# Attention with a learned position bias and a soft mixture of experts on one core: the last bias rows stored in two steps, and a 64-row bias tile read with a doubled source

## The chip, the core and the metric

One core of a Trainium2 chip runs the whole program. Its engines are PE (matmul; its weight loads are shown as PEld), DVE (vector), ACT (scalar), POOL and SP, whose queue issues every transfer of this kernel. The metric is the time on the device in microseconds, less is better.

## The reference

`q`, `k`, `v` have 8 batches, 8 heads, 576 positions and 64 dimensions. The position bias comes out of a small network with 32 hidden units and one output per head:

```python
scores = scale * np.matmul(q, k.transpose(0, 1, 3, 2))
x = (psi_rel / psi_i)[..., None]          # log1p(|i - j|) / log1p(max(i, 1))
h = np.maximum(x @ w1 + b1, 0.0)
bias = h @ w2
scores = scores + bias.transpose(2, 0, 1)[None, :, :, :]
attn = np.exp(scores - np.max(scores, axis=-1, keepdims=True))
attn = attn / (np.sum(attn, axis=-1, keepdims=True) + 1e-09)
out = np.matmul(attn, v)
```

The bias is the same for all batches and differs by head. The output of attention, 4608 tokens of 512, then goes through a soft mixture of 8 experts with 4 slots each: softmax over the tokens gathers slots, each expert is a two-layer network with weights 512 x 1024 and 1024 x 512, and a softmax over the slots spreads the results back.

## The kernel before

**Order.** Each step of the program has a name and a place in `ORDER` (line 23), a list written out by hand; steps are recorded with `step` and emitted in that order, engine by engine. A plus behind a place chooses the other engine for a step. The step `f28.3/-1` is job 28's fourth f tile, `t4.00/8` a step of unit 8.

**Bias jobs.** The bias of row i and column j depends on i and |i - j|, so 16 rows of one block make a strip of 591 values per row and head. There are 36 jobs, 8 for each block of 128 rows and 4 for the last 64 rows (`bias_job`, line 887). A job has four f tiles (ACT line 900 or DVE line 902), a product on PE (line 911) and one e tile of 128 rows (16 positions x 8 heads) x 591 (ACT line 921). Step D stores the e tile, 295.5 KB, to `bias_m` or `bias_r` in device memory (line 927). Jobs 24 to 31 make the fourth block of 128 rows, jobs 32 to 35 the last 64 rows. f and e tiles share 25 buffers (`W1N`); a buffer is free again when its last reader is done, for an e tile its store.

**Units.** A unit is one pair of heads and one batch; the 8 batches of a pair follow each other, so unit 8 begins the second pair. A unit has four blocks of 128 rows, and units of even number a fifth, the last 64 rows of two batches together in one tile of 128 partitions. For each block, PE makes scores (line 439, the fifth block line 444), DVE adds the bias and takes the extreme (line 459), ACT takes exp (line 468), POOL scales (line 374), PE transposes (line 423), and products with `v` follow (line 547).

**Bias loads.** `load_bias` (line 357) reads the bias of one pair: a bm tile of 128 rows x 1152 for each of blocks 0 to 3 (steps b0 to b3) and a br tile for the last 64 rows (b4). Both batches need the same 64 rows, so br holds them twice, in partitions 0 to 63 and 64 to 127. A tile is read in three pieces, 576 columns of the first head, then the last 64 and the first 512 of the second (line 355). The first pair's loads stand among the bias jobs' stores on SP; the other pairs' loads stand in the last units of the pair before.

**SP** works strictly in order. A load that waits for its store, or for its buffer, holds up all behind it. `load_qk` (line 343) and `load_v` (line 348) fetch the inputs of a unit into two buffers each, and `fetch_w` (line 874) fetches expert weights (wt) ahead.

Of the kernel before, what the change touches and what calls it, by code (L numbers as in the profile page):

```python
# [53 lines left out]
e4.0/2 S2.0/3 t0.10/3 m4/2 e1.0/3 t0.00/3 S2.1/3 n4.1/2 e1.1/3 t0.11/3 t2.00/3 n4.0/2 t0.01/3 t2.10/3 e0.1/3 M0/2
e0.0/3 t2.01/3 T4/2 R4/2 S3.0/3 m1/3 cR4/2+ n1.1/3 c4/2 S3.1/3 M1/2 t2.11/3 n1.0/3 Mr/2 t3.10/3 t3.11/3 t3.00/3 e2.1/3
m0/3 n0.1/3 n0.0/3 e2.0/3 e3.1/3 t3.01/3 e3.0/3 m2/3 xs/0 R1/3 xs/1 n2.0/3 x0/2 T1/3 lq/4 x1/2+ T0/3 cR1/3 m3/3 c1/3
S1.0/4 t1.10/4 t1.00/4 c0/3 n2.1/3 S1.1/4 T2/3 t1.01/4 n3.1/3 n3.0/3 lq/5 t1.11/4 S0.0/4 c2/3 S0.1/4 t0.00/4 e1.0/4
R3/3 cR3/3 T3/3 t0.10/4 t0.11/4 t0.01/4 S2.0/4 S3.0/4 c3/3 e0.0/4 e1.1/4 S3.1/4 t2.00/4 t3.00/4 t2.10/4 t3.10/4 S2.1/4
# [170 lines left out]
def body(ctx, tc, qk, v, wcol, phi, mw1, mw2, tabh, consth, *outs):  # L229
    nc = tc.nc  # L230
    P = 128
    S, D = 576, 64
# [119 lines left out]
    def read_bias(out, src, h, j0, j1):  # L352
        (row, n), (head, _), _ = src.ap
        x = bass.AP(src.tensor, src.offset + head * h + n - 1 + j0, [[row - 1, n], [1, j1 - j0]])
        nc.sync.dma_start(out=out, in_=x)
# [857 lines left out]
```

## Time and profile before

| what | value |
|---|---|
| median of 3 runs | 583.6 us (582.7 to 585.42) |
| the profiled execution | 582.65 us |
| its span, first to last instruction | 580.9 us |
| PE, DVE, ACT, POOL busy | 95%, 78%, 79%, 38% of the span |
| device memory read, written | 81.25 MB, 27.41 MB |

Times in rows of the profile are microseconds from the start of the span. A row of a timeline shows start, length, engine, line, operation, output and inputs, and in brackets the idle time of the engine just before and what ended it. SPq rows are issues of transfers; "x6" counts what is merged in a row. A row of the windows view shows a stretch, busy time of the five engines, then the granted clock of PE, the mean busy share of the 16 DMA engines and the GB/s they moved. A row of the DMA view ends with the median time from issue to landing.

### The profile page before, as it was taken

What the parts mean: (1) busy time and instruction counts of PE and PEld (TensorE: products, weight loads), DVE (VectorE), ACT (ScalarE), POOL (GpSimd) and SP (SyncE); (2) the same over time, 40 slices, a digit from 0 to 9 for tenths busy, and PEclk for the clock granted to TensorE, in tenths of its full rate; (3) what the DMA queues carried; (4) which work ended last, traced back from release to release, by engine and by line L of the source; (5) the groups of instructions that cost most, each with busy time, mean ns of one, the idle gap of its engine ahead of it and who ended that gap; (6) DMA issues with size and microseconds to landing.
All of it is one profiled execution on the core that took longest, in us unless ns stands there. A gap on an engine that the chain in (4) does not pass through costs nothing.

```text
span 580.9 us, 19319 instructions
## 1 busy us (share of the span) xinstructions
PE 549.4 (95%) x7367; PEld 354.8 (61%) x7367; DVE 454.4 (78%) x1811; ACT 459.2 (79%) x959; POOL 217.9 (38%) x308
## 2 busy tenths in 40 slices
PE   5989899999999999999999999999999999989993
PEld 3445566667766666666776666676666666543661
DVE  7998778788889788787788888888897889761333
ACT  6979889988888998988988889888879788431232
POOL 4000455555545554455544554545235331400000
PEclk9999799999999999999999999999999999999997
DMA  5598523153865254777522266430543534699978
GB/s 158 217 317 292 175 63 104 62 186 129 292 182 193 71 176 131 277 203 276 166 88 87 85 202 179 153 111 35 175 146 124 171 129 150 252 401 409 392 290 317
DMA packets 44301, 109.91 MB, mean 189 GB/s; under 512 B 8496, under 2 KB 8880, under 8 KB 44208
## 3 DMA queue, kind: packets, MB, share of 16 engines
q1 hardware_dynamic: 44208, 108.67, 54.5%
q8 instruction: 58, 0.95, 0.7%
q14 instruction: 35, 0.29, 0.2%
HBM read 81.25 MB, written 27.41 MB: 187 GB/s over the span
## 4 chain that ended last, share of the span: by engine, by line
PE 68%; DVE 11%; ACT 8%; DMA 6%; issue 4%; POOL 2%; SPq 0%; DVEq 0%; ACTq 0%; POOLq 0%
PE ps L439 18%; PE ps L547 16%; PE ps L423 14%; DVE y L459 6%; PE ps L911 4%; PE ps L444 3%; DMA xo<-xs 3%; ACT y L468 3%; PE ps L557 3%; PE ps L1037 2%; PE ps L986 2%; ACT f L900 2%; DMA qk<-in_qk_dram 2%; POOL y L374 2%; PE ps L1070 2%
## 5 line engine op out<-in xcount | busy, mean ns | idle before, releaser
L374 POOL TENSOR_SCALAR y<-y,sm 128x576 f32<-128x576 f32 x288 | 210.4, 746 | 274.8 <-DVE sm L476 220.9
L468 ACT ACTIVATE y<-y,mn 128x576 f32<-128x576 f32 x288 | 220.8, 770 | 21.2 <-DVE mn L459 16.0
L439 PE MATMUL ps<-qk 64*128 64x288 f32 x1024 | 161.3, 424 | 1.7 <-DMA qk<-in_qk_dram 0.9
L377 ACT COPY at<-ps 128x1024 f32<-128x1024 f32 (+2 forms) x151 | 132.1, 895 | 22.9 <-PE ps L423 18.8
L547 PE MATMUL ps<-at,v 128*64 128x320 f32 (+1 forms) x1024 | 133.7, 410 | 0.2 <-ACT y L468 0.2
L459 DVE CUSTOM_DVE_ANT_0 y<-ps,bm,mn 128x288 f32<-128x288 f32 x256 | 123.5, 512 | 8.8 <-PE ps L439 3.4
L423 PEld LDWEIGHTS ps<-ident,y 64*128 64x128 f32 x2592 | 100.5, 139 | 42.7 <-POOL y L374 17.0
L459 DVE CUSTOM_DVE_ANT_0 y<-ps,bm 128x288 f32<-128x288 f32 x256 | 108.2, 453 | 15.9 <-PE ps L439 9.2
L423 PE MATMUL ps<-ident,y 64*128 64x64 f32 x2592 | 113.6, 227 | 3.2 <-DVE mn L459 1.0
L439 PEld LDWEIGHTS ps<-qk 64*128 64x128 f32 x1024 | 101.3, 188 | 19.4 <-DVE mn L459 2.9
L547 PEld LDWEIGHTS ps<-at,v 128*64 128x64 f32 x1024 | 69.9, 137 | 54.5 <-DVE mn L459 6.5
L468 ACT ACTIVATION_READ_ACCUMULATOR y<-y,mn 128x1 f32 x288 | 54.8, 190 | 0.0
L475 DVE TENSOR_SCALAR sm<-sm 128x2 f32<-128x2 f32 x144 | 36.1, 251 | 20.7 <-ACT y L468 20.3
L911 PE MATMUL ps<-f,wbd 128*32 128x79 f32 (+44 forms) x640 | 44.1, 403 | 6.6 <-DVE f L902 3.9
L902 DVE TENSOR_SCALAR f<-tabs,scl,nb 128x560 f32<-128x560 f32 (+17 forms) x106 | 46.0, 507 | 2.9 <-DMA bias_m<-e 1.0
L459 DVE DVE_READ_ACCUMULATOR2_ANT mn<- 128x1 f32 x576 | 47.6, 83 | 0.0
L911 PEld LDWEIGHTS ps<-f,wbd 128*32 128x32 f32 x640 | 22.0, 113 | 28.9 <-issue 9.9
L377 DVE COPY at<-ps 128x1024 f32<-128x1024 f32 (+2 forms) x41 | 31.2, 763 | 5.4 <-PE ps L423 4.4
L900 ACT ACTIVATE f<-tabs,cols,scl 128x432 f32<-128x432 f32 (+15 forms) x38 | 26.4, 748 | 2.4 <-DMA bias_m<-e 2.4
L476 DVE RECIPROCAL sm<-sm 128x2 f32<-128x2 f32 x144 | 23.9, 166 | 4.9
L921 ACT ACTIVATE e<-ps,bcon 128x591 f32<-128x591 f32 x36 | 25.8, 762 | 1.1 <-PE ps L911 1.1
L557 PE MATMUL ps<-at,v 64*64 64x320 f32 x128 | 23.9, 448 | 0.0
(152 smaller groups left out, 434.9 us busy)
## 6 DMA issues: line engine op xcount, KB each, us to landing
wt<-in_moe_w_dram SPq DMA_DIRECT2D x62, 512.0 KB, 7.2
qk<-in_qk_dram SPq DMA_DIRECT2D x32, 576.0 KB, 4.3
bias_m<-e SPq DMA_DIRECT2D x32, 295.5 KB, 3.6
v<-in_v_dram SPq DMA_DIRECT2D x32, 288.0 KB, 4.5
xs<-xts SPq DMA_DIRECT2D x24, 288.0 KB, 3.6
xo<-xs SPq DMA_DIRECT2D x8, 864.0 KB, 4.9
bm<-bias_m SPq DMA_DIRECT2D x16, 288.0 KB, 4.4
bm<-bias_m SPq DMA_DIRECT2D x16, 256.0 KB, 4.5
```

The source lines that it names most:

```text
L374: nc.gpsimd.tensor_scalar(out=out, in0=y, scalar1=r, scalar2=1.0, op0=ALU.mult, op1=ALU.mult)
L377: (nc.vector.tensor_copy if eng else nc.scalar.copy)(out=out, in_=in_)
L423: nc.tensor.matmul(out, src[rs], ident[rs, rs], is_transpose=True, start=True, stop=True, tile_position=(64 * r, 0))
L439: nc.tensor.matmul(pss[hh].t[:, 0:HALF], x[rs, S + p * P:S + (p + 1) * P], x[rs, k0:k0 + HALF], start=True, stop=True, tile_position=(64 * ...
L459: nc.vector.tensor_tensor_reduce(out=d["y", p][:, hs], in0=d["ps", p, n][hh].read()[:, 0:HALF], in1=biases[hp][p][:, hs], scale=-QS, scala ...
L468: nc.scalar.activation(out=y, in_=y, func=AF.Exp, bias=d["mn", p][:, 2 + hh:3 + hh], scale=-1.0, accum_out=d["sm", p][:, hh:hh + 1])
L475: nc.vector.tensor_scalar(out=r, in0=r, scalar1=1e-9, scalar2=None, op0=ALU.add)
L547: nc.tensor.matmul(po.t[o:o + 64, 0:wide[c]], d["v"][:, 64 * (4 * hh + i):64 * (4 * hh + i) + 64], main[:, :, 4 * hh + i, :], start=i == 0 ...
L557: nc.tensor.matmul(d["po", c].t[o:o + 64, 0:wide[c]], d["v"][rs, 512:576], keys[c][rs], start=False, stop=True, tile_position=(64 * hh, o))
L900: nc.scalar.activation(out=f, in_=tabs[:, 0:n], func=AF.Relu, bias=cols[:, 1:2], scale=sc)
L902: nc.vector.tensor_scalar(out=f, in0=tabs[:, 0:n], scalar1=sc, scalar2=nb1[:, 0:1], op0=ALU.mult, op1=ALU.max)
L911: nc.tensor.matmul(pb.t[32 * t:32 * t + 32, a // 512, a % 512:a % 512 + c1 - c0], wbd, x, start=True, stop=True, tile_position=(0, 32 * t))
```

## The change

Three things are changed.

1. For jobs 24 to 35, step D stores only the rows of the first two heads (the first pair), in two transfers of 16 rows x 591. A new step H stores the whole e tile again, as D did before. The twelve H steps stand in `ORDER` behind `lq/3`, the load of the fourth batch's q and k.
2. The br tile is read in three transfers rather than six. The source has a leading step of zero and a count of 2, so one transfer writes all 128 partitions.
3. Jobs 0 to 23 are unchanged.

```diff
-c3/1 S2.0/2 S2.1/2 S1.1/2 t2.00/2 S3.0/2 e0.1/2 t2.10/2 S3.1/2 t2.11/2 e0.0/2 t1.11/2 m0/2 e1.1/2 t3.00/2 M1/1 t1.01/2
+H24/-1 H25/-1 H26/-1 H27/-1 H28/-1 H29/-1 H30/-1 H31/-1 H32/-1 H33/-1 H34/-1 H35/-1 c3/1 S2.0/2 S2.1/2 S1.1/2 t2.00/2
...
-    def read_bias(out, src, h, j0, j1):
+    def read_bias(out, src, h, j0, j1, twice=False):
         (row, n), (head, _), _ = src.ap
-        x = bass.AP(src.tensor, src.offset + head * h + n - 1 + j0, [[row - 1, n], [1, j1 - j0]])
+        x = bass.AP(src.tensor, src.offset + head * h + n - 1 + j0, [[0, 2]] * twice + [[row - 1, n], [1, j1 - j0]])
         nc.sync.dma_start(out=out, in_=x)
...
             x = bsp.tile([P, 2 * S], F32, name="bm", tag="bm")
-            read_bias(x[:, 0:S], bias_m[c], h0, 0, S)
-            read_bias(x[:, S:S + 64], bias_m[c], h0 + 1, 512, S)
-            read_bias(x[:, S + 64:], bias_m[c], h0 + 1, 0, 512)
+            src = bias_m[c], False
         else:
             x = bsp.tile([P, 2 * S], F32, name="br", tag="br", bufs=1)
-            for r in range(2):
-                rs = slice(64 * r, 64 * r + 64)
-                read_bias(x[rs, 0:S], bias_r, h0, 0, S)
-                read_bias(x[rs, S:S + 64], bias_r, h0 + 1, 512, S)
-                read_bias(x[rs, S + 64:], bias_r, h0 + 1, 0, 512)
+            src = bias_r, True
+        read_bias(x[:, 0:S], src[0], h0, 0, S, src[1])
+        read_bias(x[:, S:S + 64], src[0], h0 + 1, 512, S, src[1])
+        read_bias(x[:, S + 64:], src[0], h0 + 1, 0, 512, src[1])
...
+    LATE = 24
...
-        step(-1, f"D{i}", lambda _: nc.sync.dma_start(out=dst, in_=d["e"]))
+        every = dst.rearrange("p h j -> (p h) j")
+        def store(_):
+            nc.sync.dma_start(out=every, in_=d["e"])
+        def first_pair(_):
+            for h in range(2):
+                nc.sync.dma_start(out=every[h::H], in_=d["e"][h::H])
+        if i < LATE:
+            step(-1, f"D{i}", store)
+        else:
+            step(-1, f"D{i}", first_pair)
+            step(-1, f"H{i}", store)
```

On PE, DVE, ACT and POOL the same instructions stand in the same order. SP's order changes, and with it which buffer an f or e tile gets and for whom it waits.

SP before, at the end of the bias jobs (the last stores, the loads of bm and br for the first pair, then the third and fourth batches' qk and v):

```order
L927 DMA bias_m<-e 128x591 x4
L927 DMA bias_r<-e 128x591 x3
L355 DMA bm<-bias_m 128x576
L355 DMA bm<-bias_m 128x64
L355 DMA bm<-bias_m 128x512
L355 DMA br<-bias_r 64x576
L355 DMA br<-bias_r 64x64
L355 DMA br<-bias_r 64x512
...
L343 DMA qk<-in_qk_dram 128x1152 x2
L348 DMA v<-in_v_dram 128x576 x2
```

SP in the changed kernel, at the same place:

```order
L934 DMA bias_m<-e 16x591 x8
L934 DMA bias_r<-e 16x591 x6
L356 DMA bm<-bias_m 128x576
L356 DMA bm<-bias_m 128x64
L356 DMA bm<-bias_m 128x512
L356 DMA br<-bias_r 128x1x576
L356 DMA br<-bias_r 128x1x64
L356 DMA br<-bias_r 128x1x512
L344 DMA qk<-in_qk_dram 128x1152 x2
L930 DMA bias_m<-e 128x591 x8
L930 DMA bias_r<-e 128x591 x4
L349 DMA v<-in_v_dram 128x576 x2
```

Seven whole stores ahead of the loads have become fourteen small ones, br has half the transfers, and twelve whole stores stand between the qk and the v loads.

ACT before, in the bias jobs' second half, with the semaphores that each instruction waits for (a name with DMAHW is a transfer; the row of 128x384 is the step f23.3):

```order
L900 ACTIVATE f<-tabs,cols,scl 128x480 [waits DMAHW6_49,DVE_49]
L921 ACTIVATE e<-ps,bcon 128x591 [waits PE_49,Activation_49]
L921 ACTIVATE e<-ps,bcon 128x591 [waits DMAHW1_49,DVE_49,PE_49]
L900 ACTIVATE f<-tabs,cols,scl 128x384 [waits DMAHW2_49,Activation_49]
...
L900 ACTIVATE f<-tabs,cols,scl 128x448 [waits DVE_49]
...
L900 ACTIVATE f<-tabs,cols,scl 128x528
```

ACT in the changed kernel, the same instructions:

```order
L900 ACTIVATE f<-tabs,cols,scl 128x480 [waits PE_49]
L921 ACTIVATE e<-ps,bcon 128x591 [waits DVE_49,PE_49]
L921 ACTIVATE e<-ps,bcon 128x591 [waits DMAHW0_49,PE_49]
L900 ACTIVATE f<-tabs,cols,scl 128x384 [waits Activation_49]
...
L900 ACTIVATE f<-tabs,cols,scl 128x448 [waits DMAHW2_49]
...
L900 ACTIVATE f<-tabs,cols,scl 128x528 [waits DMAHW0_49]
```

The steps of 128x480 and 128x384 no longer wait for a store, those of 128x448 and 128x528 now do.

More of the change, by code (lines that the diff above doesn't have):

```diff
@@ L54 @@
[L54 to L58, printed above, removed]
@@ new lines @@
+S1.1/4 T2/3 t1.01/4 n3.1/3 n3.0/3 lq/5 t1.11/4 S0.0/4 c2/3 S0.1/4 t0.00/4 e1.0/4 R3/3 cR3/3 T3/3 t0.10/4 t0.11/4
+t0.01/4 S2.0/4 S3.0/4 c3/3 e0.0/4 e1.1/4 S3.1/4 t2.00/4 t3.00/4 t2.10/4 t3.10/4 S2.1/4 e0.1/4 m1/4 M1/3 lv/4 t3.11/4
+t3.01/4 n1.0/4 t2.11/4 n1.1/4 m0/4 e3.1/4 M0/3 n0.0/4 e3.0/4 e2.1/4 t2.01/4 e2.0/4 T1/4 n0.1/4 m3/4 T0/4 n3.1/4 R1/4
+n3.0/4 Mr/3 c1/4 cR1/4+ S4.0/4 c0/4 S4.1/4 m2/4 x0/3+ x1/3 t4.10/4 t4.00/4 T3/4 xs/3 n2.0/4 S1.0/5 t4.11/4 t4.01/4
+c3/4 S2.0/5 n2.1/4 R3/4 t1.10/5 t1.00/5 lq/7 S2.1/5 xs/2 cR3/4 S1.1/5 t2.10/5 t2.00/5 e4.0/4 e4.1/4 T2/4 S0.0/5
@@ new lines @@
+t3.01/6 e0.1/6 t2.10/6 m0/6 M1/5 n0.0/6 t3.11/6 n0.1/6 e3.0/6 e3.1/6 n1.0/6 t2.11/6 lv/6 T0/6 t2.00/6 b0/7 R1/6 Mr/5
+t2.01/6 m3/6 cR1/6+ S4.0/6 e2.1/6 e2.0/6 S4.1/6 c0/6 m2/6 x1/5+ n2.1/6 T1/6 x0/5 S0.0/7 t4.10/6 t4.00/6 S0.1/7 n3.1/6
+t4.11/6 t4.01/6 c1/6 S1.0/7 n2.0/6 t0.10/7 e4.1/6 t0.00/7 t0.11/7 n3.0/6 e4.0/6 lq/8 lv/7 t0.01/7 T3/6 R3/6 xs/5
+t1.10/7 cR3/6 m4/6 t1.00/7 S1.1/7 T2/6 S3.0/7 c3/6 n4.1/6 n4.0/6 t1.11/7 c2/6 S3.1/7 t1.01/7 S2.0/7 b2/7 t3.10/7
+e1.1/7 t3.00/7 R4/6 cR4/6+ t3.11/7 T4/6 e0.1/7 c4/6+ e0.0/7 e1.0/7 t2.00/7 S2.1/7 M0/6 m0/7 t3.01/7 lq/9 n0.0/7 M1/6
@@ new lines @@
+c0/8 t4.00/8 t4.10/8 t4.11/8 T1/8 t4.01/8 n3.0/8 n3.1/8 T2/8 c1/8 R3/8 cR3/8 S1.0/9 c2/8+ lv/8 T3/8 S0.0/9 S0.1/9
+t1.10/9 e4.1/8 c3/8 t1.00/9 e4.0/8 S1.1/9 t0.00/9 t0.10/9 t0.01/9 m4/8 n4.0/8 t0.11/9 e0.0/9 S2.0/9 S2.1/9 e0.1/9
+t1.01/9 t1.11/9 t2.00/9 m0/9 e1.0/9 n4.1/8 t2.10/9 M0/8 n0.0/9 lq/10 T4/8 R4/8 t2.01/9 S3.0/9 e1.1/9 n0.1/9 cR4/8+
+c4/8 S3.1/9 t2.11/9 T0/9 m1/9 n1.1/9 t3.00/9 t3.10/9 e2.0/9 n1.0/9 c0/9+ t3.11/9 w0/8 t3.01/9 M1/8 e2.1/9 R1/9 lv/9
+m2/9 T1/9 cR1/9+ n2.0/9 S0.0/10 S0.1/10 e3.1/9 w0/12 Mr/8 e3.0/9 m3/9 t0.10/10 t0.00/10 c1/9 n2.1/9 S1.0/10 lq/11 x1/8
@@ new lines @@
+T2/9 x0/8 n3.0/9 t0.11/10 t0.01/10 t1.10/10 n3.1/9 t1.00/10 e0.0/10 w1/12 R3/9 cR3/9+ c2/9 S2.0/10 S1.1/10 T3/9
+t2.10/10 S3.0/10 e0.1/10 t2.00/10 t1.01/10 t1.11/10 S2.1/10 S3.1/10 m0/10 t3.10/10 t3.00/10 xs/8 c3/9 n0.0/10 M0/9
+t2.01/10 n0.1/10 t2.11/10 T0/10 e1.0/10 e1.1/10 e2.1/10 m1/10 t3.11/10 n1.0/10 xs/7 e2.0/10 S4.0/10 t3.01/10 S4.1/10
+w0/10 c0/10 m2/10 n1.1/10 e3.0/10 R1/10 t4.00/10 t4.01/10 t4.10/10 e3.1/10 m3/10 n2.0/10 e4.0/10 M1/9 Mr/9 n3.1/10
+t4.11/10 cR1/10+ e4.1/10 x0/9 T1/10 S0.0/11 n3.0/10 x1/9 S0.1/11 lv/10 m4/10 n2.1/10 t0.00/11 n4.0/10 T3/10 lq/13
@@ new lines @@
+t0.10/11 c1/10 t0.01/11 R3/10 S1.0/11 t0.11/11 cR3/10 n4.1/10 T2/10 S1.1/11 c3/10 t1.00/11 t1.10/11 R4/10 S2.0/11
+t1.01/11 cR4/10 c2/10 T4/10 t1.11/11 t2.10/11 S2.1/11 e0.0/11 S3.0/11 t2.00/11 S3.1/11 t2.01/11 c4/10+ t2.11/11
+e1.1/11 e1.0/11 m1/11 M0/10 e0.1/11 t3.10/11 m0/11 t3.00/11 t3.01/11 M1/10 t3.11/11 n1.0/11 e2.0/11 n0.1/11 e2.1/11
+Mr/10 lq/12 e3.0/11 n1.1/11 T1/11 e3.1/11 x0/10 n0.0/11 lv/12 m2/11 R1/11 m3/11 x1/10 T0/11 cR1/11+ c1/11 c0/11
+S1.0/12 xs/9 n2.0/11 t1.10/12 n2.1/11 n3.1/11 t1.00/12 S1.1/12 t1.11/12 t1.01/12 n3.0/11 T2/11 S0.0/12 T3/11 c2/11
@@ new lines @@
+t0.10/12 R3/11 lv/11 w0/11 w1/11 t0.00/12 S2.0/12 cR3/11+ S2.1/12 c3/11 t2.10/12 t2.00/12 e1.0/12 S0.1/12 S3.0/12
+S3.1/12 t0.01/12 e1.1/12 t0.11/12 M1/11 t3.10/12 m1/12 e0.0/12 e0.1/12 t2.01/12 t3.11/12 m0/12 t2.11/12 n1.0/12
+n1.1/12 e3.1/12 e2.0/12 M0/11 n0.1/12 t3.00/12 t3.01/12 n0.0/12 e3.0/12 R1/12 T1/12 S4.0/12 m3/12 Mr/11 n3.1/12
+n3.0/12 cR1/12+ e2.1/12 m2/12 c1/12 n2.1/12 S4.1/12 t4.00/12 n2.0/12 lq/15 xs/10 T3/12 t4.10/12 x0/11 x1/11+ t4.11/12
+t4.01/12 S1.0/13 R3/12 T0/12 c3/12 cR3/12+ S2.0/13 t1.00/13 t1.10/13 S2.1/13 c0/12 xs/11 e4.0/12 S1.1/13 e4.1/12 T2/12
@@ new lines @@
+t2.10/13 t2.00/13 S0.0/13 t2.11/13 c2/12 t1.11/13 S0.1/13 e1.1/13 t1.01/13 m4/12 e1.0/13 t0.10/13 t2.01/13 n4.1/12
+t0.00/13 n4.0/12 t0.01/13 m1/13 M0/12 T4/12 R4/12 S3.0/13 cR4/12+ S3.1/13 e0.0/13 t0.11/13 w1/16 lq/14 n1.0/13
+t3.10/13 t3.00/13 c4/12 M1/12 e0.1/13 e2.0/13 t3.11/13 m0/13 e2.1/13 n1.1/13 n0.1/13 Mr/12 n0.0/13 t3.01/13 T0/13
+m2/13 e3.0/13 R1/13 n2.1/13 x0/12+ e3.1/13 n2.0/13 T1/13 x1/12+ cR1/13+ m3/13 c0/13 n3.1/13 S1.0/14 S3.0/14 T2/13
+c1/13 S1.1/14 n3.0/13 xs/12 t1.10/14 t1.00/14 T3/13 t3.00/14 t3.10/14 c2/13 lv/13 w0/13 w1/13 t1.11/14 R3/13 t1.01/14
@@ new lines @@
+cR3/13+ S2.0/14 c3/13 S0.0/14 S3.1/14 t2.00/14 e1.0/14 t0.00/14 t0.10/14 w0/14 S0.1/14 S2.1/14 t0.11/14 t0.01/14 M1/13
+e1.1/14 t2.10/14 e0.0/14 m1/14 t2.01/14 n1.0/14 M0/13 t2.11/14 e0.1/14 n1.1/14 e2.0/14 b1/15 m0/14 t3.01/14 n0.0/14
+n0.1/14 t3.11/14 T1/14 R1/14 e2.1/14 cR1/14+ Mr/13 e3.0/14 e3.1/14 c1/14 S4.0/14 S4.1/14 m2/14 lv/14 m3/14 t4.00/14
+t4.10/14 t4.01/14 x1/13 w1/15 n2.1/14 n2.0/14 t4.11/14 n3.1/14 T0/14 x0/13 c0/14 S0.0/15 S0.1/15 n3.0/14 t0.10/15
+T2/14 t0.00/15 R3/14 S3.0/15 e4.0/14 t0.11/15 cR3/14+ t0.01/15 e4.1/14 t3.00/15 T3/14 t3.10/15 m4/14 c2/14 c3/14
@@ new lines @@
+S1.0/15 e0.0/15 S1.1/15 S3.1/15 e0.1/15 n4.1/14 t1.00/15 lq/17 S2.0/15 t1.10/15 n4.0/14 t1.11/15 S2.1/15 b4/15
+t1.01/15 T4/14 t3.01/15 c4/14+ M0/14 t3.11/15 m0/15 b0/15 R4/14 e3.0/15 t2.10/15 t2.11/15 e1.1/15 e1.0/15 t2.00/15
+m1/15 e3.1/15 lq/16 b2/15 e2.1/15 n0.1/15 w1/14 t2.01/15 n0.0/15 M1/14 m3/15 cR4/14 Mr/14 b3/15 e2.0/15 n1.0/15 T0/15
+x0/14 x1/14 m2/15 n1.1/15 R1/15 cR1/15+ n3.0/15 S1.0/16 T1/15 c0/15 S0.0/16 c1/15 t1.10/16 S1.1/16 n2.1/15 t1.00/16
+n3.1/15 t0.00/16 t0.10/16 n2.0/15 S0.1/16 t1.11/16 R3/15 T2/15 t1.01/16 lv/15 cR3/15 T3/15 c2/15 S2.0/16 t0.01/16
@@ L331, in body @@
             jobs.append((bases, [4 * len(jobs) + t for t in range(4)],
[L332 removed]
+                         dst[:, :, (112 if c < 4 else 48) - 16 * m:][:, :, 0:S + 15]))
     units = [(hp, b) for hp in range(NP) for b in range(B)]
```

82 lines of the change are left out of this document (21 added, 61 removed).

## The prediction

> **What bounds the kernel now.** I read the page first, for the bound over the whole run, then the chain of waits, which names where the first 70 us are lost, then the timelines of PE, DVE and SP (the queue that issues every transfer) at the places that the change touches.
>
> ```profile
> span 580.9 us, 19319 instructions
> PE 549.4 (95%) x7367; PEld 354.8 (61%) x7367; DVE 454.4 (78%) x1811; ACT 459.2 (79%) x959; POOL 217.9 (38%) x308
> PEclk9999799999999999999999999999999999999997
> PE 68%; DVE 11%; ACT 8%; DMA 6%; issue 4%; POOL 2%; SPq 0%; DVEq 0%; ACTq 0%; POOLq 0%
> ```
>
> PE is busy 95% and carries 68% of the chain, so whatever makes PE stand moves the end by about as much. Only one slice inside the run has a lower clock, the fifth: the passage from the bias jobs to attention. In the chain the stretch ahead of it reads (start, us, what):
>
> ```profile
> 38.97 4.22 DMA bias_m<-e
> 43.27 0.71 ACT f L900
> 44.03 3.23 PE ps L911 x46
> ```
>
> A store of bias rows ends a wait of ACT, and ACT ends one of PE. The timelines of ACT and PE give the idle time in brackets:
>
> ```profile
> 43.27 0.71 ACT L900 ACTIVATE f<-tabs,cols,scl 128x384 f32<-128x384 f32 x1 [2.37 <-DMA bias_m<-e]
> 38.65 4.07 PE L911 MATMUL ps<-f,wbd 128*32 128x336 f32 x52 [0.81 <-DVE f L902]
> 44.03 3.23 PE L911 MATMUL ps<-f,wbd 128*32 128x384 f32 x52 [1.31 <-ACT f L900]
> ```
>
> ACT waited 2.37 us for a buffer that a store still read. PE lost 1.31 us by it, and 0.81 us before.
>
> **The first part: stores cut and put off.** Jobs 24 to 35 now store a quarter of their rows (two heads of eight) in two transfers of 16 rows; the whole 295.5 KB follow later. Ahead of the bias loads this takes 12 x 0.75 x 295.5 KB = 2.66 MB off the queues. The rate when full stands in the windows view (last two columns: share of the 16 DMA engines, GB/s):
>
> ```profile
> 42.00:44.00 2.00, 0.72 (x7) 0.02 (x1) 1.55 (x5) 0.73 (x2) 0.00 (x0) 1.00 1.03 397
> ```
>
> At 397 GB/s that is 6.7 us of transfer time, but the engines wait for little of it. The ACT step above no longer waits for a store (the order in the section on the change shows it), so its 2.37 us go, and PE gets back at most 1.31 + 0.81 = 2.1 us; at least nothing, if f tiles now wait on other stores, since 12 e tiles keep their buffers. I take 1.3, the gap directly behind this wait.
>
> At the end of the phase DVE waits for the two last bias tiles:
>
> ```profile
> 63.73 0.46 DVE L459 CUSTOM_DVE_ANT_0 y<-ps,bm 128x288 f32<-128x288 f32 x1 [0.62 <-DMA bm<-bias_m]
> 67.45 0.46 DVE L459 CUSTOM_DVE_ANT_0 y<-ps,br 128x288 f32<-128x288 f32 x1 [0.34 <-DMA br<-bias_r]
> 55.91 2.13 SPq L927 DMA_DIRECT2D bias_r<-e  x3
> 59.24 1.28 SPq L355 DMA_DIRECT2D bm<-bias_m  x3
> 61.53 3.67 SPq L355 DMA_DIRECT2D br<-bias_r  x6
> 68.78 7.42 SPq L343 DMA_DIRECT2D qk<-in_qk_dram  x2
> 78.91 13.04 SPq L348 DMA_DIRECT2D v<-in_v_dram  x2
> ```
>
> The bm load comes earlier by the bias phase's 1.3 us and a queue emptier of stores, so the 0.62 us go; I count 0.6. What happens to br is the second part.
>
> The 12 whole stores stand between the two qk loads (the second issued at about 76 us) and the v load of 78.91. They are 3.55 MB, 8.9 us at 397 GB/s, so that v load lands near 90 instead of 82. Its first use is the third unit's M0, at 97:
>
> ```profile
> 97.01 1.95 PE L547 MATMUL ps<-at,v 128*64 128x256 f32 x16
> ```
>
> So they cost nothing; without that cover, a few us. The 24 small issues on SP replace 12; SP then works for about 0.35 us each (the last 3 issues took 2.13 us with a wait in them) while it waits for ACT's e tiles anyway: 0.
>
> **The second part: br in 3 transfers, not 6.** Four times per run. Three issues less save SP about 3 x 0.6 us each time (3.67 us for six); that hides behind the loads. What may cost is the shape. The old loads begin with 64 rows, all other transfers with 64 or 128. The new source begins with a step of zero and a count of 2. If a transfer is dealt out by its first count, each br transfer runs on 2 of the 16 engines, 64 rows each. No row of this trace shows such a transfer, so the price has two ends: nothing (spread as now: 576 KB at 397 GB/s, 1.5 us for the three), or 397 / 16 = 24.8 GB/s per engine and 64 x (2304 + 256 + 2048) bytes = 295 KB on each of two: 11.9 us. I take the second end. The traces don't decide it; I lean on the shape, since an even deal of 128 rows needs a first count that divides among 16.
>
> The Trainium skill, "DMA: Bandwidth & Descriptors", section "Why a DMA increments its semaphore by 16 and not by 1", says that a transfer from SP uses the largest number of engines up to 16 that divides both sides' slowest dimension, and the same page's section "Rules for kernel authors" names a leading zero-stride broadcast of c copies as confined to at most c engines. By that rule the sum is the 606 us below, and without it 581.7; no run here shows it so far.
>
> *First pair.* The stores of job 35 are issued when SP's three at 55.91 end, at about 58.0; the two small ones land some 2 us later (5 KB took 1.6, the large ones 3.6), less 1.3 for the earlier phase: br is issued from about 59.1.
>
> ```profile
> cols<-in_wcol_dram SPq DMA_DIRECT2D x1, 5.0 KB, 1.6
> bias_m<-e SPq DMA_DIRECT2D x32, 295.5 KB, 3.6
> ```
>
> With 1.6 + 11.9 us and some 0.4 for the short rows it lands at 73.0. DVE needs both its last parts at 67.45: +5.5 us against before, with the gain of 1.3 already in it.
>
> *Second pair.* Issue, landing (of the six: least, median, most), and DVE's first uses:
>
> ```profile
> 157.99 4.18 SPq L355 DMA_DIRECT2D br<-bias_r  x6
> DMA to landing us min/median/max: 5.6/7.1/8.0
> 168.90 0.45 DVE L459 CUSTOM_DVE_ANT_0 y<-ps,br 128x288 f32<-128x288 f32 x1
> 169.27 0.45 DVE L459 CUSTOM_DVE_ANT_0 y<-ps,br 128x288 f32<-128x288 f32 x1
> ```
>
> The sixth, issued at 161.6, landed at about 167.2. With 11.9 instead of 1.5 us on the engines it is 177.6; the second use waits 8.3 us.
>
> *Third pair.* br itself is used 20 us later; what suffers is what stands behind it on the two engines:
>
> ```profile
> 248.68 4.63 SPq L355 DMA_DIRECT2D br<-bias_r  x6
> 253.41 1.48 SPq L355 DMA_DIRECT2D bm<-bias_m  x3
> 254.99 0.38 SPq L343 DMA_DIRECT2D qk<-in_qk_dram  x1
> 255.46 1.32 SPq L355 DMA_DIRECT2D bm<-bias_m  x3
> 262.10 0.46 DVE L459 CUSTOM_DVE_ANT_0 y<-ps,bm 128x288 f32<-128x288 f32 x1 [1.09 <-DMA bm<-bias_m]
> ```
>
> DVE already waits at 262.10 for a bm part issued at 255.46. If the two engines start br at about 251, they end at 263, and with 3.7 us for bm, qk and that part (576, 576 and 288 KB at 397 GB/s) and 0.6 to land, it is there at about 267.5. The upper end is the full 10.4 us. I take 6.
>
> *Fourth pair.* The same order of loads, with more slack:
>
> ```profile
> 352.92 4.26 SPq L355 DMA_DIRECT2D br<-bias_r  x6
> 357.28 5.05 SPq L355 DMA_DIRECT2D bm<-bias_m  x9
> 368.26 0.45 DVE L459 CUSTOM_DVE_ANT_0 y<-ps,bm 128x288 f32<-128x288 f32 x1
> ```
>
> Started near 354.5, br holds the two engines to 366.4, the first six bm parts to 369.5; against 368.26 this is 1 to 7 us; I take 2.5.
>
> These waits are DVE's. PE runs on for about 1 us with what is queued, so 3 us come off over the places. On the other side a PE that stands is slowed afterwards, as in the passage (the column ahead of the last two is the clock):
>
> ```profile
> 62.00:64.00 2.00, 1.54 (x8) 0.71 (x8) 0.84 (x5) 2.00 (x5) 1.07 (x3) 0.60 0.59 181
> 66.00:68.00 2.00, 2.00 (x34) 1.66 (x34) 1.26 (x8) 1.98 (x4) 0.73 (x2) 0.50 0.22 71
> 68.00:70.00 2.00, 2.00 (x18) 1.03 (x12) 1.25 (x6) 1.27 (x2) 1.46 (x3) 0.69 0.23 30
> ```
>
> There some 3.4 us of busy PE from 66 on ran at half clock, which costs about 1.7 us. Two new such stretches: +3.
>
> **The sum.** 5.5 + 8.3 + 6 + 2.5 - 3 + 3 = 22.3. The profiled execution took 582.65 us (580.9 of span and 1.75 around it): 605.0. The median of the runs shown, 583.6, lies 0.95 above it: forecast 606.0.
>
> **The rivals.** *Spread as before, and faster.* If the three br transfers run on all engines, only the first part's effect is left: -1.3 - 0.6, 581.7 us as a median, from 578 (both PE gaps of 2.1, the waits of 0.62 and 0.34, and the low clock of the passage gone, 1.7) to 583. It decides as soon as br lands within 8 us of its issue in the first two pairs. For it speaks that six transfers at 157.99 share one queue without trouble; against it only the shape. Chance 0.16.
>
> *The gain is eaten, no change.* The 12 held e tiles leave 13 of 25 buffers for f and e until the late stores. Steps of ACT that waited for no store now do (the order shows two at rows of 128x448 and 128x528), and if one of them is as late as the old one, the 2.37 us are only moved. With br spread: 583.6, from 582 to 585. Against it: the stores it waits for are older and whole, ahead of the small ones. Chance 0.10.
>
> *Confined* (the forecast): 0.74. Its own range is 595 to 617: below, when the third and fourth pair are covered and PE runs on longer (5.5 + 8.3 - 2 = 11.8); above, with their upper ends of 10.4 and 7.
>
> **How the numbers follow.** About 0.5%, 2.9 us, is what a measurement of this kernel can tell from no change. Confined is all slower: 0.74, and 0.01 from the eaten gain: 0.75. Of spread, half lies below 580.7: 0.08. The rest, 0.17, is the same. The range leaves out the gain below 583 (about 0.11 of spread) and the tails of confined: 583 to 617.
>
> **What would show it.** Right: the br transfers land 12 us or more after issue, and DVE has a wait of over 5 us on br near 66 and another near 175; ACT's 2.37 us on bias_m<-e are gone; the first bm wait of 0.62 too; the late stores bring no new wait on v at 97. The rates show it too: with br alone in flight the DMA share falls to about an eighth. Wrong: br landing in 3 us, with no wait; then the time is near 582. If the waits stand but the end moves less, PE had more queued than 1 us.

## The result and the profile after

| | median | runs |
|---|---|---|
| before | 583.15 us | 582.48 to 585.42 (4) |
| changed | 619.94 us | 617.55 to 620.39 (4) |

The ratio is 1.0618, 95% interval 1.0577 to 1.0659. The forecast was 606.0 us with a range of 583 to 617: the direction holds, the time lies above the range, and the loss is 37 us where 22 were forecast. Each ratio below is to the kernel before, measured beside that run, with its 95% interval. One execution of a later run, `lead4`, took 1035 us and is left out of that run's figures. The profiled execution of the changed kernel has a span of 618.1 us, 37.2 longer than before. Its page:

```profile
PE 559.0 (90%) x7367; PEld 362.8 (59%) x7367; DVE 454.0 (73%) x1811; ACT 460.4 (74%) x959; POOL 218.4 (35%) x308
PE 62%; DMA 11%; DVE 10%; ACT 9%; issue 3%; SPq 1%; POOL 1%; DVEq 0%; ACTq 0%; POOLq 0%
```

PE runs the same 7367 matmuls. It is busy 9.6 us longer (559.0 against 549.4, at a lower clock in places) and stands 27.6 us longer. In the chain, transfers rise from 6% to 11%. The view of waits names what DVE and PE wait for: DVE three times for bm (18.1 us in total) and twice for br (15.9), PE once for a qk load (8.2). Two waits are on br itself. Three on bm and one on qk are on transfers that are not slow by their own shape. DVE's timeline gives its five places:

```profile
66.24 0.46 DVE L457 CUSTOM_DVE_ANT_0 y<-ps,bm 128x288 f32<-128x288 f32 x1 [4.69 <-DMA bm<-bias_m]
79.44 0.46 DVE L457 CUSTOM_DVE_ANT_0 y<-ps,br 128x288 f32<-128x288 f32 x1 [9.81 <-DMA br<-bias_r]
187.19 0.46 DVE L457 CUSTOM_DVE_ANT_0 y<-ps,br 128x288 f32<-128x288 f32 x1 [6.14 <-DMA br<-bias_r]
289.42 0.46 DVE L457 CUSTOM_DVE_ANT_0 y<-ps,bm 128x288 f32<-128x288 f32 x1 [9.20 <-DMA bm<-bias_m]
400.90 0.46 DVE L457 CUSTOM_DVE_ANT_0 y<-ps,bm 128x288 f32<-128x288 f32 x1 [4.22 <-DMA bm<-bias_m]
```

DVE runs the same instructions in the same order in both kernels, so the start of one instruction after, minus its start before, is the delay collected so far. That makes a ledger of the loss:

| instruction (start before) | start after | delay | added |
|---|---|---|---|
| last bm of the first pair (63.73) | 66.24 | 2.5 | 2.5 |
| first br (67.45) | 79.44 | 12.0 | 9.5 |
| second pair, second br (169.27) | 187.19 | 17.9 | 5.9 |
| third pair, first bm (262.10) | 289.42 | 27.3 | 9.4 |
| fourth pair, first bm (368.26) | 400.90 | 32.6 | 5.3 |
| end of the span (580.9) | 618.1 | 37.2 | 4.6 |

The chain after gives the slow transfers at these places (start of issue, us to landing):

```profile
64.26 14.94 DMA br<-bias_r
...
171.03 16.03 DMA br<-bias_r
...
277.73 10.17 DMA qk<-in_qk_dram
...
392.28 8.46 DMA bm<-bias_m
```

The third br piece lands 15 to 16 us after its issue begins. Before, the six pieces of the first pair took, by the view of the tile:

```profile
DMA to landing us min/median/max: 2.4/2.7/2.9
```
The rate after, while br is alone (last three columns: clock, DMA share, GB/s):

```profile
76.00:78.00 2.00, 0.00 (x0) 0.00 (x0) 0.00 (x0) 0.00 (x0) 0.00 (x0) 0.50 0.13 49
```

0.13 is two engines of sixteen, 24.5 GB/s each: the forecast's second end (24.8). The windows view also shows what a stand does to PE: after the wait at 400.90 it is busy all the time, at half clock.

```profile
402.00:404.00 2.00, 2.00 (x11) 1.84 (x11) 1.70 (x8) 0.93 (x3) 0.00 (x0) 0.50 0.97 325
```

SP at the first pair:

```profile
51.14 6.31 SPq L934 DMA_DIRECT2D bias_m<-e  x8
57.50 3.75 SPq L934 DMA_DIRECT2D bias_r<-e  x6
61.35 1.47 SPq L356 DMA_DIRECT2D bm<-bias_m  x3
63.01 3.52 SPq L356 DMA_DIRECT2D br<-bias_r  x3
```

Fourteen small stores occupy SP for 10 us in a row, some 0.63 us each in the second row, and the last bm load is issued at 61.35, later than before (59.24), although the bias jobs ended earlier: ACT finishes the last e tile at 56.2 us (57.7 before), and SP issues its last store at 60.7 (57.7 before).

### The profile page after: what moved, and what is told of

The parts are those of the page before. It is cut to its first block, busy times and chain, and to the rows that moved or that the text cites. A ratio compares the mean times of both kernels' runs of the same rounds, so it can differ in the third digit from the quotient of the medians.

```text
span 618.1 us, 19325 instructions
## 1 busy us (share of the span) xinstructions
PE 559.0 (90%) x7367; PEld 362.8 (59%) x7367; DVE 454.0 (73%) x1811; ACT 460.4 (74%) x959; POOL 218.4 (35%) x308
## 4 chain that ended last, share of the span: by engine, by line
PE 62%; DMA 11%; DVE 10%; ACT 9%; issue 3%; SPq 1%; POOL 1%; DVEq 0%; ACTq 0%; POOLq 0%
PE ps L437 17%; PE ps L545 14%; PE ps L421 12%; DVE y L457 5%; DMA br<-bias_r 5%; ACT y L466 4%; PE ps L911 3%; PE ps L999 3%; ACT f L900 3%; PE ps L442 2%; PE ps L1050 2%; PE ps L555 2%; DMA xo<-xs 2%; DMA qk<-in_qk_dram 2%; PE ps L1083 2%
## 5 line engine op out<-in xcount | busy, mean ns | idle before, releaser
L437 PE MATMUL ps<-qk 64*128 64x288 f32 x1024 | 167.4, 435 | 21.8 <-DVE mn L457 13.2
L457 DVE CUSTOM_DVE_ANT_0 y<-ps,bm 128x288 f32<-128x288 f32 x256 | 108.4, 453 | 35.2 <-DMA bm<-bias_m 18.1
L421 PEld LDWEIGHTS ps<-ident,y 64*128 64x128 f32 x2592 | 102.0, 141 | 52.5 <-POOL y L372 15.0
L437 PEld LDWEIGHTS ps<-qk 64*128 64x128 f32 x1024 | 105.8, 194 | 40.0 <-DVE mn L457 16.2
L421 PE MATMUL ps<-ident,y 64*128 64x64 f32 x2592 | 115.3, 229 | 12.0 <-DVE mn L457 10.1
L911 PE MATMUL ps<-f,wbd 128*32 128x512 f32 (+44 forms) x640 | 43.1, 402 | 6.1 <-DVE f L902 4.1
L911 PEld LDWEIGHTS ps<-f,wbd 128*32 128x32 f32 x640 | 23.3, 112 | 26.2 <-issue 9.6
L375 DVE COPY at<-ps 128x1024 f32<-128x1024 f32 (+2 forms) x41 | 31.2, 763 | 6.2 <-PE ps L421 5.9
L457 DVE CUSTOM_DVE_ANT_0 y<-ps,br 128x288 f32<-128x288 f32 x32 | 13.6, 453 | 21.0 <-DMA br<-bias_r 15.9
## 6 DMA issues: line engine op xcount, KB each, us to landing
bias_m<-e SPq DMA_DIRECT2D x32, 295.5 KB
```

The lines of the kernel that those rows point to most:

```text
L375: (nc.vector.tensor_copy if eng else nc.scalar.copy)(out=out, in_=in_)
L421: nc.tensor.matmul(out, src[rs], ident[rs, rs], is_transpose=True, start=True, stop=True, tile_position=(64 * r, 0))
L437: nc.tensor.matmul(pss[hh].t[:, 0:HALF], x[rs, S + p * P:S + (p + 1) * P], x[rs, k0:k0 + HALF], start=True, stop=True, tile_position=(64 * ...
L457: nc.vector.tensor_tensor_reduce(out=d["y", p][:, hs], in0=d["ps", p, n][hh].read()[:, 0:HALF], in1=biases[hp][p][:, hs], scale=-QS, scala ...
L911: nc.tensor.matmul(pb.t[32 * t:32 * t + 32, a // 512, a % 512:a % 512 + c1 - c0], wbd, x, start=True, stop=True, tile_position=(0, 32 * t))
```

## The experiments

### One part at a time

`six_reads` is the changed kernel with this edit:

```diff
...
-            src = bias_r, True
...
+            for r in range(2):
+                rs = slice(64 * r, 64 * r + 64)
+                read_bias(x[rs, 0:S], bias_r, h0, 0, S)
+                read_bias(x[rs, S:S + 64], bias_r, h0 + 1, 512, S)
+                read_bias(x[rs, S + 64:], bias_r, h0 + 1, 0, 512)
```

> The changed kernel, with br read in six transfers of 64 rows again: the first part alone. Theory (the doubled source is confined to two DMA engines, and that makes nearly all of the loss): the waits of 9.81 and 6.14 us on br and of 9.20 and 4.22 us on the bm tiles behind it are gone. What is left is the passage: the bias jobs end 1.2 us earlier, but SP still needs about 0.6 us for each small store, so the wait of 4.69 us on bm stays, and br comes about 2 us later than before: 585.6 us, 584 to 587.5. Rival (the held buffers, the small stores and the late stores cost most of it): 600 or more, with the waits in other places than br. Second rival (the tail's 2.2 us and the passage belong to the first part as well): 588.

Measured: 584.46 us against 584.84, ratio 1.0002 (0.9971 to 1.0033). No wait on br is left. The wait on bm is, as SP and DVE show:

```profile
56.21 3.75 SPq L937 DMA_DIRECT2D bias_r<-e  x6
60.06 1.47 SPq L356 DMA_DIRECT2D bm<-bias_m  x3
```

```profile
65.25 0.46 DVE L460 CUSTOM_DVE_ANT_0 y<-ps,bm 128x288 f32<-128x288 f32 x1 [4.34 <-DMA bm<-bias_m]
```

DVE comes to this wait 2.2 us earlier than before (65.25 - 4.34 against 63.73 - 0.62) and leaves it 1.5 us later; its span, 581.0 us, is that of before (580.9). So the first part makes no difference that can be told (its interval allows 0.3% either way, some 2 us), and both rivals of this run fall.

`double_only` is the kernel before with this edit:

```diff
-            for r in range(2):
-                rs = slice(64 * r, 64 * r + 64)
-                read_bias(x[rs, 0:S], bias_r, h0, 0, S)
...
+            src = bias_r, True
...
```

> The kernel before, with br read in three transfers with the doubled source: the second part alone. Theory: issue at 61.5 as before, then some 16 us to land, first use at about 77.5 rather than 67.45 (+10); second pair +6.5, third +9, fourth +6, tail 0 to 2: 615 us, 611 to 620, with a DMA share near 0.13 while br is alone in flight. Rival (the first part costs most): 583 to 590.

Measured: 618.12 us, ratio 1.0575 (1.0521 to 1.0629), inside its expected 611 to 620. The second part alone makes the loss; its interval overlaps the changed kernel's, so that no loss of the first part can be told from these runs. The chain and SP at the first pair:

```profile
62.65 15.05 DMA br<-bias_r
```

```profile
61.43 6.13 SPq L355 DMA_DIRECT2D br<-bias_r  x3
```

From the first issue to the last landing it takes 62.65 + 15.05 - 61.43 = 16.3 us. In the changed kernel it is 64.26 + 14.94 - 63.01 = 16.2.

### The zero step or the first count

`lead2` and `lead4` are the kernel before, with six transfers of 64 rows and no doubling. Only the place of the rows in device memory is changed: 64 unused elements stand behind every 32 (16) rows, so that the source needs two row dimensions, 2 x 32 (4 x 16). The lines are those of lead4:

```diff
-    bias_r = dram.tile([64, H, S + 64], F32, name="bias_r")
+    bias_r = dram.tile([4, 16 * H * (S + 64) + 64], F32, name="bias_r")
...
+        x = bass.AP(bias_r.tensor, bias_r.offset + head * h + 63 + j0, [[group - 16, 4], [row - 1, 16], [1, j1 - j0]])
```

> The kernel before, its bias_r padded by 64 elements behind every 32 rows, so that each of the six transfers of 64 rows has a source that begins with a count of 2 and a step that is not zero (2 x 32 rows). No doubling, as many transfers and bytes as before. Theory (the first count of the source sets how many DMA engines share a transfer): 295 KB on each of two engines as in the changed kernel, 612 to 620 us, with waits on br of about 10 and 6 us. Rival (it is the zero step, two reads of the same rows, that is slow): 583 to 585, no waits.

> As lead2, but padded behind every 16 rows, so that the first count is 4. Theory: 147 KB on each of four engines, 5.9 us of transfer where two take 11.9 and sixteen 1.5. First pair +4.4, second +2.3 (it had 2.1 us of slack), third +4.4, fourth 0, clock 1: 595 us, 590 to 600, DMA share near 0.25 while br is alone. Rival (zero step): 583 to 585. Second rival (every shape with two row dimensions is confined to two engines, whatever the count): as lead2.

Measured: lead2 623.71 us, ratio 1.0667 (1.0612 to 1.0723); lead4 592.0 us (the median of its three other executions), ratio 1.0129 (1.0067 to 1.0192). `lead4_again` is lead4 once more, for a profile.

> lead4 once more, for a profile of an execution like the three others: 591 to 594 us. Theory of four engines: DVE waits 3 to 5 us on br in the first pair and 1 to 3 in the second, a DMA share of 0.25 while br is alone, and less than 2 us at the third pair.

Measured: 595.17 us, one execution, above its expected 594. Of lead4_again, DVE's wait, SP, the chain, and the rate in two microseconds in which no other load of the kernel is in flight:

```profile
71.08 0.46 DVE L464 CUSTOM_DVE_ANT_0 y<-ps,br 128x288 f32<-128x288 f32 x1 [4.45 <-DMA br<-bias_r]
```

```profile
61.30 3.42 SPq L360 DMA_DIRECT2D br<-bias_r  x6
```

```profile
64.21 6.71 DMA br<-bias_r
```

```profile
66.00:68.00 2.00, 1.96 (x24) 0.91 (x20) 0.33 (x2) 2.00 (x4) 1.21 (x2) 0.54 0.32 107
```

The DMA view of the same stretch (packets, MB, share of the 16 engines) shows that not all of this is br: one packet fetches instructions.

```profile
q1 hardware_dynamic: 111, 0.20, 26.1%
q8 instruction: 1, 0.02, 5.9%
```

Without that packet of some 16 KB, 8 GB/s in these two microseconds, br has about 98 GB/s and 26% of the 16 engines: four engines at 24.5 GB/s each, the same rate for an engine as in the changed kernel.

And of lead2:

```profile
76.78 0.46 DVE L464 CUSTOM_DVE_ANT_0 y<-ps,br 128x288 f32<-128x288 f32 x1 [10.50 <-DMA br<-bias_r]
```

```profile
64.00:66.00 2.00, 1.71 (x32) 1.53 (x30) 1.61 (x10) 1.84 (x5) 0.00 (x0) 0.50 0.14 49
```

A first count of 2 without a zero step gives 49 GB/s and much the same wait; a count of 4 gives about 98 GB/s and a wait of 4.45 us where 3 to 5 were expected. (lead4's first expectation, +4.4, was of the delay against before, which is 71.08 - 67.45 = 3.6.) So the first count sets the number of engines, and the zero step is not needed. lead4 has no wait on br in the second pair (1 to 3 were expected), and at the third PE waits 4.2 us for the qk load (4.4 by its first expectation, under 2 by its second). lead2 lies above its expected 620, and above double_only with the same bytes on two engines; by the ledger most of these 5.6 us are added from the third pair on (the second pair's second br starts at 186.97 against 186.06, the spans end at 623.2 against 617.1). Why was not tried. The Trainium skill, "DMA: Bandwidth & Descriptors", section "Why a DMA increments its semaphore by 16 and not by 1", lets the slowest dimensions of both sides decide, with the largest divisor up to 16. The 49 and 98 GB/s at counts of 2 and 4 agree with it.

### The same three transfers, spread

`spread128` is the kernel before with three transfers for br as in the changed kernel, but the 64 rows are stored twice, the second copy shifted by 64 elements, so that one step runs through 128 rows:

```diff
-        x = bass.AP(src.tensor, src.offset + head * h + n - 1 + j0, [[row - 1, n], [1, j1 - j0]])
+        n -= 65 * twice
+        x = bass.AP(src.tensor, src.offset + head * h + n - 1 + j0, [[row - 1, n + 64 * twice], [1, j1 - j0]])
...
+            if i >= 32:
+                row = H * (S + 64)
+                at = bias_r.offset + 64 * (row - 1) + 16 * (i - 32) * row + 48 - 16 * (i - 32)
+                nc.sync.dma_start(out=bass.AP(bias_r.tensor, at, [[S + 64, P], [1, S + 15]]), in_=d["e"])
```

> The kernel before, with br in three transfers as in the changed kernel, but out of rows that stand twice in device memory, the second copy shifted so that one step of rows runs through all 128: the source's first count is 128 rather than 2, with the same bytes into the same tile. For it jobs 32 to 35 are stored twice, 1.18 MB more ahead of the loads of the first pair. Theory (the first count is all that makes the changed kernel's br slow): no waits of more than 1 us on br in pairs 2 to 4, the first pair up to 2 later by the extra stores: 584 to 587 against a before of 584.5. Rival (128 rows in one transfer into this tile are slow in themselves): 600 or more.

Measured: 585.73 us against 583.73, ratio 1.0025 (0.9985 to 1.0066), as expected. The view of the br tile and SP at the second pair:

```profile
DMA to landing us min/median/max: 2.6/4.1/6.3
```

```profile
160.87 2.41 SPq L356 DMA_DIRECT2D br<-bias_r  x3
```

With 128 as the first count, the same three transfers of the same bytes into the same tile land in 2.6 to 6.3 us and nothing waits for them. So the first count accounts for the slow transfers. It also shows no gain of three transfers over six: SP saves 1.8 us at the second pair (4.18 to 2.41), and nobody waited for it. The Trainium skill, "DMA: Bandwidth & Descriptors", section "Rules for kernel authors", advises one transfer of 128 partitions for two to disjoint halves, because they share the same engines. No run here shows a gain from that: 1.0025 with the extra stores.

### What stands behind the slow transfer

At the third pair DVE never waits for br, and yet 9 us are lost. `third_only` doubles the source for that pair alone:

```diff
-            for r in range(2):
-                rs = slice(64 * r, 64 * r + 64)
-                read_bias(x[rs, 0:S], bias_r, h0, 0, S)
+            for r in range(1 if hp == 2 else 2):
+                rs = slice(0, P) if hp == 2 else slice(64 * r, 64 * r + 64)
+                read_bias(x[rs, 0:S], bias_r, h0, 0, S, hp == 2)
...
```

> The kernel before, with the doubled source for the third pair alone. There br's first use comes 25 us after its issue, and DVE never waited for br at this place in the changed kernel. Theory (what stands behind br on its two engines pays): PE waits about 8 us for the qk load of unit 16 and DVE about 9 for the bm tile at the same place, and a low clock costs 1 to 2 behind it: +10, some 594 to 595 us against a before of about 584.5. Rival (only a late br costs): no change, 584.5.

Measured: 593.93 us, ratio 1.0161 (1.0118 to 1.0204), as the theory had it. PE's and DVE's timelines:

```profile
269.37 1.33 PE L439 MATMUL ps<-qk 64*128 64x288 f32 x4 [8.31 <-DMA qk<-in_qk_dram]
```

```profile
270.85 0.46 DVE L459 CUSTOM_DVE_ANT_0 y<-ps,bm 128x288 f32<-128x288 f32 x1 [9.32 <-DMA bm<-bias_m]
```

`third_behind` moves the same slow load behind the bm tiles and that qk load:

```diff
-b4/15 t1.01/15 T4/14 t3.01/15 c4/14+ M0/14 t3.11/15 m0/15 b0/15 R4/14 e3.0/15 t2.10/15 t2.11/15 e1.1/15 e1.0/15
+t1.01/15 T4/14 t3.01/15 c4/14+ M0/14 t3.11/15 m0/15 b0/15 R4/14 e3.0/15 t2.10/15 t2.11/15 e1.1/15 e1.0/15
...
-t2.00/15 m1/15 e3.1/15 lq/16 b2/15 e2.1/15 n0.1/15 w1/14 t2.01/15 n0.0/15 M1/14 m3/15 cR4/14 Mr/14 b3/15 e2.0/15
+t2.00/15 m1/15 e3.1/15 lq/16 b2/15 e2.1/15 n0.1/15 w1/14 t2.01/15 n0.0/15 M1/14 m3/15 cR4/14 Mr/14 b3/15 b4/15 e2.0/15
```

> As third_only, and step b4/15 moved behind b3/15, so that the same slow br transfers are issued behind the three bm tiles and the qk load of unit 16, at about 257 us. Theory: nothing that is needed soon stands behind them; br lands about 16 us later, at 273, and its first use is at 273.8: 0 to 2 us of wait, 584.5 to 587. Rival (the slow transfers slow the others wherever they stand, or hold SP so long that the v loads come late): 590 or more.

Measured: 594.11 us, ratio 1.0174 (1.0133 to 1.0214). My theory expected next to no loss; the rival with the v loads was right. The long waits on bm and qk are gone (0.9 us on qk is left, as before), and another has come, as PE and SP show:

```profile
277.08 6.28 PE L547 MATMUL ps<-at,v 128*64 128x320 f32 x32 [11.18 <-DMA v<-in_v_dram]
```

```profile
257.50 8.47 SPq L355 DMA_DIRECT2D br<-bias_r  x3
266.02 3.14 SPq L348 DMA_DIRECT2D v<-in_v_dram  x1
```

```profile
266.02 10.93 DMA v<-in_v_dram
```

SP needs 8.5 us for three issues, so the v load starts at 266.0, and it takes 10.9 us to land, as the chain in the last fence shows. Before, SP issued it at 261.2, and the v loads issued there took 5.6 to 6.6 us to land:

```profile
261.17 0.33 SPq L348 DMA_DIRECT2D v<-in_v_dram  x1
```
I had looked only at what stood ahead, and had not asked what stands behind in the new place. Here the loss moved with the slow transfer to the load that now follows it: 4.9 us by the late issue, 4 to 5 by the slow landing.

### A lighter first part

`late8` is six_reads with only jobs 24 to 31 stored in two steps:

```diff
-H24/-1 H25/-1 H26/-1 H27/-1 H28/-1 H29/-1 H30/-1 H31/-1 H32/-1 H33/-1 H34/-1 H35/-1 c3/1 S2.0/2 S2.1/2 S1.1/2 t2.00/2
+H24/-1 H25/-1 H26/-1 H27/-1 H28/-1 H29/-1 H30/-1 H31/-1 c3/1 S2.0/2 S2.1/2 S1.1/2 t2.00/2
...
-        if i < LATE:
+        if i < LATE or i >= 32:
```

> The first part alone (br in six transfers), with only jobs 24 to 31 stored in two steps; jobs 32 to 35 store the whole tile at once, as before. So 16 small stores in place of 24, and six fewer between job 31 and the load of b3. Theory (in six_reads the bias phase won 1.8 us, and SP's 0.6 us for each small store, 14 of them in a row ahead of b3, took it back): b3 is issued about 2.7 us earlier, at 57.4, its wait of 4.3 us falls to under 1.5 and the time to 582.5 against a before of 584.5, a ratio of 0.995 to 0.999. Rival (the stores' traffic, not SP, made b3 late, or the whole stores of 32 to 35 hold br back): 1.000 or above.

Measured: 583.53 us against 584.44, ratio 0.999 (0.9965 to 1.0014), no difference that can be told. SP and DVE:

```profile
57.34 1.56 SPq L933 DMA_DIRECT2D bias_r<-e  x3
59.09 1.94 SPq L356 DMA_DIRECT2D bm<-bias_m  x3
```

```profile
64.95 0.46 DVE L460 CUSTOM_DVE_ANT_0 y<-ps,bm 128x288 f32<-128x288 f32 x1 [2.48 <-DMA bm<-bias_m]
```

Six small stores have become three whole ones, and SP saves 2.2 us (3.75 to 1.56). The load is issued 1.0 us earlier than in six_reads (at 59.09, where 57.4 was expected) and the wait falls by 1.9 us, to 2.48 where under 1.5 was expected. DVE's use itself starts only 0.3 us earlier (64.95 against 65.25), because DVE came to it 1.6 us later: ACT waits 1.40 us for a store at 42.93 us, 0.29 us at the same step in six_reads. The ratio lies at the edge of the theory's 0.995 to 0.999, and its interval holds the rival's 1.000 too. What speaks for SP's issue time is how long the last store is issued after its e tile is done: 3.9 us in six_reads (55.5 and 59.4), 1.4 in late8 (57.1 and 58.5), nothing before (57.7 and 57.7). No version tried beats the kernel before by a measurable amount.

## Why the prediction was right in kind and wrong in size

**The first count confines br to two engines.** Right, by the rates of 49 and 98 GB/s, by lead2 and lead4, and against spread128. Both rivals fall for the changed kernel, since br is not spread in it. The outcome of the second, a gain that is eaten, came true for the first part alone (six_reads, 1.0002), but by another cause than the one given: SP's issues ate it, while ACT's longest wait for a store is 0.29 us there.

**The sizes.** The forecast's terms against the ledger. What the ledger adds between the end of one wait and the next, 4.4 us, is the low clock less what PE's running on has saved. PE's running on, 2.8, is read off PE's rows below, and the low clock is the rest, 7.2.

| term | forecast | measured |
|---|---|---|
| first pair, with the first part | +5.5 | +12.0 |
| second pair | +8.3 | +5.9 |
| third pair | +6 | +8.5 |
| fourth pair | +2.5 | +4.4 |
| PE runs on | -3 | -2.8 |
| low clock behind the waits | +3 | +7.2 |
| the tail | 0 | +2.0 |
| sum | +22.3 | +37.2 |

The 4.4 are 0.9, 0.9 and 2.6 behind the second, third and fourth pairs: the delay at the rows of 173.05, 263.12 and 376.98 us of before, less the ledger's at the wait ahead of each. Before:

```profile
173.05 0.46 DVE L459 CUSTOM_DVE_ANT_0 y<-ps,bm 128x288 f32<-128x288 f32 x1
...
263.12 0.46 DVE L459 CUSTOM_DVE_ANT_0 y<-ps,bm 128x288 f32<-128x288 f32 x1 [0.17 <-POOL y L374]
...
376.98 0.46 DVE L459 CUSTOM_DVE_ANT_0 y<-ps,br 128x288 f32<-128x288 f32 x1
```

After:

```profile
191.87 0.46 DVE L457 CUSTOM_DVE_ANT_0 y<-ps,bm 128x288 f32<-128x288 f32 x1 [0.71 <-PE ps L437]
...
291.32 0.46 DVE L457 CUSTOM_DVE_ANT_0 y<-ps,bm 128x288 f32<-128x288 f32 x1 [1.06 <-issue]
...
412.23 0.46 DVE L457 CUSTOM_DVE_ANT_0 y<-ps,br 128x288 f32<-128x288 f32 x1 [2.55 <-PE ps L442]
```

The forecast is short by 14.9 us, and no single term makes that: the first pair lacks 6.5, the low clock 4.2, the third pair 2.5, the tail 2.0, the fourth pair 1.9, while the second pair was put 2.4 too high. The range's upper end stands on the upper ends of the third and fourth pairs alone (5.5 + 8.3 + 10.4 + 7 - 3 + 3 = 31.2, which gives 614.8); the first pair and the clock, which failed most, had none.

**The step that failed most is the first pair's: the 24 small issues on SP were put at 0.** I counted 0.35 us for each and let SP wait for the e tiles anyway. They take about 0.6 us, and fourteen stand in a row ahead of the last two loads, so br was issued at 63.0, not 59.1: 3.9 of the 6.5 us. The rest is the landing: 16.2 us from the first issue, where I had 1.6 + 11.9 + 0.4. lead4 gives a second point: 64.21 + 6.71 - 61.30 = 9.6 us for half the bytes on each engine (5.95 us at the full rate). Both runs lie on a line of 3.0 us and 1.1 times the transfer time: a start that costs more than the 1.6 us of a 5 KB load, and about a tenth more than the full rate gives. That split is an estimate from two points. Before, br is issued at 61.53. So of the 3.9 us of late issue, 2.4 are a gain that did not come, and 1.5 a loss by the small stores.

**The second failed step is the low clock: "Two new such stretches: +3".** PE does run on, as forecast. After:

```profile
79.96 2.29 PE L437 MATMUL ps<-qk 64*128 64x288 f32 x8 [9.01 <-DVE mn L457]
...
187.71 0.47 PE L421 MATMUL ps<-ident,y 64*128 64x64 f32 x4 [5.31 <-DVE mn L457]
...
287.94 1.33 PE L437 MATMUL ps<-qk 64*128 64x288 f32 x4 [8.19 <-DMA qk<-in_qk_dram]
...
401.42 4.58 PE L437 MATMUL ps<-qk 64*128 64x288 f32 x16 [3.67 <-DVE mn L457]
```

PE stands 9.01, 5.31 and 3.67 us where DVE waits 9.81, 6.14 and 4.22. At the third pair it waits for the qk load itself, 7.5 us longer than before (8.19 against 0.66), and DVE 8.1 (9.20 against 1.09). That is 0.8, 0.8, 0.6 and 0.6 us less, 2.8 in all. But PE loses this and more as soon as it resumes. Before, at the first, third and fourth of these places:

```profile
68.64 1.51 PE L439 MATMUL ps<-qk 64*128 64x288 f32 x8
...
261.20 0.76 PE L439 MATMUL ps<-qk 64*128 64x288 f32 x4 [0.66 <-DMA qk<-in_qk_dram]
...
368.71 2.65 PE L439 MATMUL ps<-qk 64*128 64x288 f32 x20
```

The same eight matmuls take 2.29 us instead of 1.51, four take 1.33 instead of 0.76, and sixteen take 4.58 where twenty took 2.65, with no idle time inside these rows. The granted clock is 0.50 behind each of the four stands (80 to 82, 188 to 190, 288 to 290 and 402 to 404 us). So four stretches cost some 7.2 us, where two at 3 were forecast; 7.2 is what the ledger leaves for them, not a sum of rows.

**Second pair.** The 8.3 counted the transfer from the sixth issue at 161.6. With three transfers it begins at the first (169.69 in SP's row after, 157.99 before), and the last piece lands at 171.03 + 16.03 = 187.1. Less the 11.7 us of delay so far that is 175.4, not 177.6.

**Third and fourth pairs.** The mechanism, loads queued behind br, is right by third_only; 8.5 and 4.4 lie inside the bounds of 10.4 and 1 to 7, above the values taken. SP's hold, which the prediction did not have, is in them: before, the first qk load of the third pair was issued at 254.99, 6.3 us after br's first issue; after, at 277.73, 9.8 us behind the 267.89 of SP's row.

```profile
267.89 5.85 SPq L356 DMA_DIRECT2D br<-bias_r  x3
```

**The first part.** ACT's wait of 2.37 us is gone; this row is the longest that is left there:

```profile
42.00 0.84 ACT L900 ACTIVATE f<-tabs,cols,scl 128x544 f32<-128x544 f32 x1 [0.37 <-DMA bias_m<-e]
```

DVE comes to the last bm tile 1.6 us earlier (66.24 - 4.69 against 63.73 - 0.62), 1.3 was forecast. Some of that may be the execution: third_behind, whose bias phase is that of before, comes there 0.9 us earlier too (62.88 - 0.70). "The 0.62 us go" is wrong: it became 4.69, because SP, not the queue, was late. The late stores at 88 us cost nothing, as forecast: no wait on v is in the view of waits. The rival's gain of 1.9 us for spread transfers is not there either, by six_reads. (The forecast took a KB of the views as 1000 bytes. A stored tile of 128 x 591 x 4 bytes, 295.5 KB in the views, has 302,592, so the late stores are 3.63 MB and 9.1 us rather than 3.55 and 8.9; no term changes by it.)

**The tail** was not in the forecast. Some 2 us are added ahead of the experts, where PE runs at half clock for about seven microseconds:

```profile
558.00:560.00 2.00, 2.00 (x12) 0.39 (x8) 0.00 (x0) 0.00 (x0) 0.00 (x0) 0.50 1.02 408
```

The same stretch is at half clock in the profiled executions of double_only, lead2, third_only and lead4_again, and at full clock in before, six_reads, late8, spread128 and third_behind. Between DVE's instructions at 520.24 and 528.55 us of before, the five with the half clock lose 1.4 to 2.1 us and the others under 0.1. What sets it off is not settled.

## What to carry to other kernels

A source that begins with a small count can save issues and cost the engines: look at the first count before counting transfers, and price such a transfer by its bytes per engine. Its victims are also the loads behind it, and moving it changed the victim here; ask at the new place who follows. Price a stand of the busiest engine together with the low clock behind it. Cutting a store into small ones is paid for by the queue that issues them, and that price comes due where the next load stands in the same queue.
